# Loading queries and storing outputs of two token groups by one transfer each, in a fused attention and SoLU feed-forward kernel

## The chip, the cores and the metric

The kernel runs on one core of a Trainium2 chip. The metric is the device time of one execution in microseconds (us). TensorE is called PE here, VectorE DVE, ScalarE ACT, GpSimd POOL, and SyncE SP; SP computes nothing and issues nearly all of the DMAs, in the order of the program.

## The reference

Four batches of 12288 queries attend to 768 pooled keys, and each result row goes through a feed-forward layer with a SoLU activation and a layer norm.

```python
kv_pool = kv.reshape(B, H//4, 4, W//4, 4, C).mean(axis=(2, 4))     # B=4, 768 keys of C=128
k = v = kv_pool.reshape(B, -1, C) @ w_sr
s = (q @ k.transpose(0, 2, 1)) / sqrt(C)                           # q: (4, 12288, 128)
a = softmax(s);  x = (a @ v).reshape(B * 12288, C)
h = x @ w_in                                                       # d_ff = 1024
solu = h * softmax(h)
ln = (solu - mean) / sqrt(var + 1e-6) * g_ln
out = ln @ w_out                                                   # (49152, 128), float32
```

## The kernel before

The 49152 query rows are 384 tiles of 128 rows. Four tiles make a group (GT = 4), so there are 96 groups (NG), 24 to a batch. One long loop has 384 slots, and every slot issues one step of each stage of a software pipeline, for tiles that lie further back the later the stage is. In slot t the scores of tile t+1 are computed (`scores_pe`, L386: six matmuls of 384 columns, with the queries split into a high and a low part), the row maximum, exponential and the split of the probabilities of tile t (L402, L403, L407, L415), the product with the values for a whole group in four quarters (`values`, L453), the first feed-forward matmul of tile t-9 (`hidden_pe`, L505), its activation (L513, L529, L543), and the second feed-forward matmul of tile t-13 (`final_pe`, L631: 24 matmuls of 128 columns).

Two operands are turned by DMA transposes that SP issues: the probabilities, 384 KB a tile, from `phl` into `pT` (L422), and the activations, 512 KB a tile, from `uhl` into `uT` (`hidden_turn`, L580). `uhl` is written by two POOL instructions (L560, L566) on `u` of DVE. `final_pe` of a tile stands two slots behind its `hidden_turn`, and `uT` has four buffers. So every slot asks for one transpose of each kind, and over four slots SP also issues one load of queries (`q_load`, L345, 256 KB, at the end of each slot with slot % 4 == 3) and one store of outputs (`final_store`, L685, 256 KB, in each slot with slot % 4 == 1). While batches 1 to 3 are prepared, which is during the three batches before the last, SP also loads raw keys and values, 384 KB at a time (`kv_load`, L216, 64 in all), POOL adds them up (`kv_add`, L227), and some matmuls and transposes of keys are set between the others. In the last batch, from about 1295 us on, none of that is left.

The queries of group g are loaded five slots or more ahead of `q_split` (L354, ACT) and `q_low` (L362, POOL), which split them into `qh` and `ql`; `scores_pe` also reads `qf` itself as bfloat16. `qf` has three buffers of 512 columns, so a load waits until the scores of the group three before have been read. `final_half` (L674, DVE) scales half a group of outputs out of PSUM into `ob`, which has two buffers; the second half is computed in the slot of the store, just ahead of it.

The order of the work on every engine is written out by hand; semaphores are put in by the framework, which gives the DMAs eight completion semaphores in turn. At the start SP's queue holds the two weight matrices, sixteen chunks of the first batch's keys and values (`kv_first_load`, 384 KB each) with the first queries after the sixth chunk, then the queries of groups 1 and 2, and six chunks of batch 1. The last four groups are stored by another function (`final_mul`, `TAIL`), which the change leaves alone.

Of the kernel before, what the change touches and what calls it, by code (L numbers as in the profile page):

```python
# [11 lines left out]
F32 = mybir.dt.float32  # L12
F32R = mybir.dt.float32r
F16 = mybir.dt.float16
BF16 = mybir.dt.bfloat16
# [6 lines left out]
P = 128  # L22
# [10 lines left out]
GT = 4  # L33
GPB = TPB // GT
NG = NT // GT
# [42 lines left out]
def kernel(  # L78
# [15 lines left out]
    nc = tc.nc  # L94

    dmt = ctx.enter_context(tc.tile_pool(name="dmt", bufs=2))
# [45 lines left out]
    state = {}  # L142
# [20 lines left out]
    def kv_first_load(half, c):  # L163

        n = half * 8 + c
        tag, bufs = ("kvc", 9) if n < 9 else ("uT", 4) if n < 13 else ("uhl", 3)
        t = dmt.tile([P, 2, 384], F32, tag=tag, name=f"kv_{half}_{c}", bufs=bufs)
        nc.sync.dma_start(t, kv0[:, 2 * c : 2 * c + 2, half * 384 : half * 384 + 384])
        state["kv0", half, c] = t
# [165 lines left out]
            yield slot, [partial(f, b, half) for f in fs]  # L335


    QL = 1

    def q_load(g):  # L340
        if g >= NG or g % QL:
            return
        b, gb = divmod(g, GPB)
        t = dmt.tile([P, QL * 512], F32, tag="qf", name=f"qf_{g}", bufs=3)
        nc.sync.dma_start(t, qT[b, :, gb * 512 : (gb + QL) * 512])  # L345
        state["qf", g // QL] = t

    def q_split(g):
        if g >= NG:
            return  # L350
        qf = state["qf", g // QL][:, (g % QL) * 512 : (g % QL + 1) * 512]
        qh = grp.tile([P, 512], F32R, tag="qh", name=f"qh_{g}")
        ql = grp.tile([P, 512], BF16, tag="ql", name=f"ql_{g}")
        nc.scalar.copy(qh, qf)  # L354
        state["q", g] = (qh, ql)

    def q_low(g):
        if g >= NG:
            return
        qf = state["qf", g // QL][:, (g % QL) * 512 : (g % QL + 1) * 512]  # L360
        qh, ql = state["q", g]
        nc.gpsimd.tensor_tensor(ql, qf, qh.bitcast(F32), op=ALU.subtract)  # L362

# [3 lines left out]
    def scores_pe(t):  # L367
        g, j = divmod(t, GT)
        b = t // TPB
        qh, ql = state["q", g]  # L370
        qt = state["qf", g // QL].bitcast(BF16).rearrange("p (n two) -> p n two", two=2)[:, :, 1]
        kh, kl, kc = (state[n, b] for n in ("kh", "kl", "kc"))
        ts = slice(j * P, (j + 1) * P)
        s = ps_r.tile([P, 2, 512], F32, tag="r", name=f"s_{t}")
        if t in PY:
            py = s[:, 0, 384:385]
            for half in range(2):
                nc.tensor.matmul(
                    py, onesm, state["kss", PY[t]][:, half : half + 1], start=half == 0, stop=half == 1
                )  # L380
            state["py", PY[t]] = py
        row = [(n, half, *x) for n, x in enumerate(((ql, kc), (qh, kh), (qt, kl))) for half in range(2)]
        if t == 0:
            row = sorted(row[2:4] + row[:2] + row[4:], key=lambda x: x[1])
        for n, half, lh, rh in row:
            nc.tensor.matmul(  # L386
                s[:, half, :384],
                lh[:, ts],
                rh[:, half * 384 : (half + 1) * 384],
                start=n == (t == 0),  # L390
                stop=n == 2,
            )
        state["s", t] = s[:, :, :384]
# [274 lines left out]

    def final_half(g, half):
        _, f = state["f", g]  # L670
        if half == 0:
            state["ob", g, 0] = dmt.tile([P, GT, P], F32, tag="ob", name=f"ob_{g}_0")
        js = slice(half * 2, half * 2 + 2)
        nc.vector.scalar_tensor_tensor(  # L674
            state["ob", g, 0][:, js],
            state["po", g][:, half * 256 : half * 256 + 256].rearrange("p (j c) -> p j c", j=2),
            swi,
            f[:, js].unsqueeze(2).to_broadcast([P, 2, P]),
            op0=ALU.mult,
            op1=ALU.mult,  # L680
        )

    def final_store(g, j0=0, j1=GT):
        t0, n = g * GT + j0, j1 - j0
        nc.sync.dma_start(  # L685
            out[t0 * P : (t0 + n) * P, :].rearrange("(j p) c -> p j c", p=P),
            state.pop(("ob", g, j0)),
        )

    def final_out(g):  # L690
        final_half(g, 1)
        final_store(g)


    ident = const.tile([P, P], F32, name="ident")
# [32 lines left out]
    for n in range(16):  # L728
        if n == OUT_AT:
            nc.sync.dma_start(raw_out, w_out.bitcast(I32))  # L730
        if n == Q_AT:
            q_load(0)
        kv_first_load(*divmod(n, 8))
    q_load(1)
    q_load(2)
    for pos in SOON:
        kv_load(1, pos)
# [36 lines left out]
    nc.vector.tensor_scalar(wsc, wsc, 2.0**14, None, op0=ALU.mult)  # L774
    nc.scalar.activation(w_in_h, wf, AF.Copy, scale=wsc)
    q_split(0)
    q_low(0)
    for f in out_steps[4:]:
        f()
# [63 lines left out]
    def w_low():  # L843
        nc.gpsimd.tensor_tensor(wcl, gw, wch, op=ALU.subtract)

    fill = {
        0: [partial(q_split, 1), partial(q_low, 1), w_mean, w_center],
        1: [busy],
        2: [partial(kv_bound, 0, 1), partial(kv_bound, 0, 2), busy],
# [38 lines left out]
    for b in range(1, B):  # L888
        for k, fs in kv_plan(b):
            plan.setdefault((b - 1) * TPB + k, []).append(fs)  # L890
    scores_pe(0)
    for slot in range(NT):
        i = slot - LH
# [17 lines left out]
        if 0 <= av < NG:  # L911
            values(av, qtr, 0)
        at(slot + 1, scores_pe)
        at_soon(slot - NORM, values_norm)
        at_last(slot - FSC, final_scale)
# [3 lines left out]
        if slot < NT and 0 < qs < slot and (slot - 1 - qs) % GT == 0:  # L919
            q_low(slot // GT + 1)  # L920
# [26 lines left out]
        at_soon(slot - NORM, values_recip_u)  # L947
        at(i + 1, hidden_pe)
        at_last(slot - LO, final_half, 0)
        if slot < NT - 1:  # L950
            at(slot - LO, final_pe)
        if late:
            values(av, qtr, 1)
        at(i - 1, hidden_turn)
        at_last(slot - LO - 1, final_out)
        at_last(slot - XSP, values_out)
        for st in todo:
# [10 lines left out]
        if slot < NT and 0 < qs <= slot and (slot - qs) % GT == 0:  # L968
            q_split(slot // GT + 1)
# [61 lines left out]
```

## Time and profile before

| | |
|---|---|
| three runs, median (lowest to highest) | 1851.75 us (1847.76 to 1853.61) |
| profiled execution, first to last instruction | 1847.1 us; 4.65 us less than the median |
| busy: PE, DVE, ACT, POOL | 1821.1, 1784.9, 1752.8, 1613.8 us |
| DMA | 431.80 MB, mean 234 GB/s |
| DMA issues of SP | 384 `pT`, 378 `uT`, 64 `kv`, 96 `qf`, 97 `out` (two of them smaller) |
| granted TensorE clock | 1.00 in all slices |

The profile is of one execution and has a span alone; its own time with what lies around the span is not listed apart, so the span stands beside the median of the runs. A busy share is the time in which an engine had an instruction in work; ends of matmuls are modelled. For a DMA, the time to landing runs from its issue on SP until its last completion.

### The profile page before, as it was taken

The page shows a single profiled execution, that of the slowest core. Times are in us where ns is not written, and L with a number is a line of the kernel's source. Part 1 is how long each engine was busy: PE and PEld are TensorE (multiplying, and loading weights), DVE is VectorE, ACT ScalarE, POOL GpSimd, SP SyncE. Part 2 cuts the span into 40 slices and gives each one's busy share as a digit, 9 for nine tenths or more (in the row PEclk, how much of TensorE's full clock was granted, in tenths as well). Part 3 has the DMA queues.
Part 4 walks back from the last instruction along what each step waited for, and adds up shares of the span by engine and source line. Part 5 has one row for each costly group of instructions (what it writes and reads, how often), then busy time and mean ns, then how long its engine had stood idle before and what let it go on. Part 6 is the DMA issues. An engine that isn't in the chain of part 4 may idle for free.

```text
span 1847.1 us, 43152 instructions
## 1 busy us (share of the span) xinstructions
PE 1821.1 (99%) x15717; PEld 1179.2 (64%) x15718; DVE 1784.9 (97%) x2729; ACT 1752.8 (95%) x3148; POOL 1613.8 (87%) x1392
## 2 busy tenths in 40 slices
PE   8999999999999999999999999999999999999999
PEld 4566666666666666666666666666666666666666
DVE  7999999999999999999999999999999999999998
ACT  6999999999999999999999999999999999999998
POOL 3899889899998999989988899989888888888887
PEclk9999999999999999999999999999999999999999
DMA  8999999999999999999999999999999999999998
GB/s 300 208 238 233 229 245 234 236 240 245 232 234 240 244 238 241 235 233 238 235 233 234 247 241 241 238 236 231 227 217 230 233 228 223 230 227 231 224 223 179
DMA packets 1473253, 431.80 MB, mean 234 GB/s; under 512 B 1400977, under 2 KB 1454353, under 8 KB 1472785
## 3 DMA queue, kind: packets, MB, share of 16 engines
q1 hardware_dynamic: 1472752, 428.98, 114.1%
q8 instruction: 124, 2.03, 0.5%
q14 instruction: 89, 0.72, 0.1%
q10 hardware_dynamic: 288, 0.07, 0.0%
HBM read 52.50 MB, written 25.17 MB: 42 GB/s over the span
## 4 chain that ended last, share of the span: by engine, by line
PE 63%; DVE 13%; ACT 7%; POOL 7%; issue 7%; DMA 3%; DVEq 0%; POOLq 0%; ACTq 0%
PE o L631 19%; PE h L505 18%; PE xa L453 13%; PE s L386 13%; DVE junkd L513 3%; DVE nm L402 3%; POOL uhl L566 3%; DVE phl L415 2%; ACT e L529 2%; DMA pT<-phl 2%; ACT junk L603 2%; POOL uhl L560 2%; ACT phl L407 2%; DVE u L543 1%; DVE ob L674 1%
## 5 line engine op out<-in xcount | busy, mean ns | idle before, releaser
L566 POOL TENSOR_TENSOR uhl<-u,uhl 128x1024 f16<-128x1024 f32 x382 | 815.1, 2134 | 31.7 <-ACT uhl L558 0.2
L631 PEld LDWEIGHTS <-uT 128*128 128x128 f16 x9072 | 537.1, 98 | 91.9 <-DMA uT<-uhl 7.0
L631 PE MATMUL o<-wch,uT 128*128 128x128 f16 x6048 | 568.0, 219 | 1.3 <-DMA uT<-uhl 1.3
L631 PE MATMUL o<-wcl,uT 128*128 128x128 f16 x3024 | 525.9, 219 | 0.0
L560 POOL TENSOR_SCALAR uhl<-u 128x1024 f16<-128x1024 f32 x377 | 393.5, 1044 | 136.2 <-DVE u L543 131.1
L543 DVE SCALAR_TENSOR_TENSOR u<-h,rz,e 128x1024 f32<-128x1024 f32 x384 | 491.2, 1279 | 16.0 <-ACT e L529 3.6
L513 DVE TENSOR_SCALAR_CACHE_REDUCE junkd<-h,rz 128x1024 bf16<-128x1024 f32 x384 | 491.5, 1280 | 1.4 <-PE h L505 1.0
L529 ACT ACTIVATE e<-h,nm,rz 128x1024 f32<-128x1024 f32 x384 | 459.0, 1195 | 1.0 <-DVE junkd L513 1.0
L603 ACT ACTIVATE junk<-u,su 128x1024 bf16<-128x1024 f32 x384 | 437.8, 1140 | 0.2 <-DVE u L543 0.2
L402 DVE TENSOR_REDUCE nm<-s 128x1 f32<-128x768 f32 x384 | 365.7, 952 | 23.3 <-PE s L386 20.8
L453 PE MATMUL xa<-pT,vh 128*128 128x512 f16 x1152 | 373.5, 379 | 6.6 <-DMA pT<-phl 4.0
L403 ACT ACTIVATE s<-s,nm 128x768 f32<-128x768 f32 x384 | 335.9, 875 | 41.9 <-DVE nm L402 37.1
L415 DVE SCALAR_TENSOR_TENSOR phl<-s,phl 128x768 f16<-128x768 f32 x384 | 366.3, 954 | 4.5 <-ACT phl L407 4.3
L407 ACT ACTIVATE phl<-s 128x768 f16<-128x768 f32 x384 | 311.0, 810 | 11.7
L505 PEld LDWEIGHTS <-xh 128*128 128x128 f16 x1536 | 144.8, 97 | 191.7 <-issue 26.7
L386 PE MATMUL s<-kh,qh 128*128 128x384 f32 x768 | 248.0, 404 | 0.1
L505 PE MATMUL h<-w_in_h,xh 128*128 128x512 f16 x768 | 228.2, 379 | 3.5 <-DVE rz L487 2.4
L505 PE MATMUL h<-w_in_h,xl 128*128 128x512 f16 x768 | 228.4, 379 | 0.0
L505 PE MATMUL h<-w_in_l,xh 128*128 128x512 f16 x768 | 228.3, 379 | 0.0
L453 PE MATMUL xa<-pT,vl 128*128 128x512 f16 x576 | 218.3, 379 | 0.0
L386 PE MATMUL s<-kc,ql 128*128 128x384 bf16 x768 | 187.8, 326 | 7.4 <-DVE phl L415 4.4
L386 PE MATMUL s<-kl,qf 128*128 128x384 bf16 x768 | 192.2, 332 | 0.1
(127 smaller groups left out, 1707.2 us busy)
## 6 DMA issues: line engine op xcount, KB each, us to landing
kv<-in_kv_dram SPq DMA_DIRECT2D x64, 384.0 KB, 4.3
qf<-in_q_dram SPq DMA_DIRECT2D x96, 256.0 KB, 3.3
out_dram<-ob SPq DMA_DIRECT2D x95, 256.0 KB, 2.8
pT<-phl SPq DMA_TRANSPOSE x384, 3.8
uT<-uhl SPq DMA_TRANSPOSE x378, 4.4
raw_in<-in_moe_w_in_dram SPq DMA_DIRECT2D x1, 1024.0 KB, 5.4
raw_out<-in_moe_w_out_dram SPq DMA_DIRECT2D x1, 1024.0 KB, 8.6
out_dram<-ob SPq DMA_DIRECT2D x1, 192.0 KB, 2.0
```

The source lines that it names most:

```text
L386: nc.tensor.matmul(s[:, half, :384], lh[:, ts], rh[:, half * 384 : (half + 1) * 384], start=n == (t == 0), stop=n == 2,)
L402: nc.vector.tensor_reduce(nm, s, axis=AX.XY, op=ALU.max, negate=True)
L415: nc.vector.scalar_tensor_tensor(phl[:, 1], state.pop(("s", t)), SC, phl[:, 0], op0=ALU.mult, op1=ALU.subtract)
L453: nc.tensor.matmul(xa, v[:, c, :], pT[:, :, a * NKC + c, :], start=n == 0, stop=n == len(seq) - 1)
L505: nc.tensor.matmul(h[:, hs], lh[:, ts], rh[:, hs], start=n == 0, stop=n == 2)
L513: nc.vector.tensor_scalar(junk, state["h", t], state["rz", g][1][:, j : j + 1], None, op0=ALU.mult, op1=ALU.min, accum_out=nm,)
L529: nc.scalar.activation(e, state["h", t], AF.Exp, bias=nm, scale=state["rz", g][0][:, js], accum_out=state["z2", g][:, js],)
L543: nc.vector.scalar_tensor_tensor(u, state.pop(("h", t)), state["rz", g][2][:, j : j + 1], state.pop(("e", t)), op0=ALU.mult, op1=ALU.mult, ...
L560: nc.gpsimd.tensor_scalar(uhl[:, 0, :], u, 1.0, 1.0, op0=ALU.mult, op1=ALU.mult)
L566: nc.gpsimd.tensor_tensor(uhl[:, 1, :], u, uhl[:, 0, :], op=ALU.subtract)
L603: nc.scalar.activation(junk, u, AF.Square, scale=-float(DFF), bias=su, accum_out=state["v3", g][:, j : j + 1],)
L631: nc.tensor.matmul(po[:, ts], uT[:, a * NFC + c, :], w[:, c, :], start=start, stop=stop)
```

## The change

`q_load` loads the queries of two groups at once, 512 KB, into a tile of 1024 columns with two buffers (before: 512 columns and three). It is called in the same places and does nothing for an odd g. Only groups 0 and 1 are still loaded apart, into the two halves of one tile. The outputs of two groups are gathered in a tile `ob2` of 512 KB with one buffer (before: 256 KB and two), and one DMA stores them behind the second half of the odd group. Thus the loads of the loop stand in the slots with slot % 8 == 7, and the stores in those with slot % 8 == 5. `qf` takes 2048 bytes more of each partition, `ob2` 4096 more beside `ob`, which the tail still uses.

```diff
-    def q_load(g):
-        if g >= NG or g % QL:
+    def q_load(g, n=2):
+        if g >= NG or n == 2 and g % 2:
             return
         b, gb = divmod(g, GPB)
-        t = dmt.tile([P, QL * 512], F32, tag="qf", name=f"qf_{g}", bufs=3)
-        nc.sync.dma_start(t, qT[b, :, gb * 512 : (gb + QL) * 512])
-        state["qf", g // QL] = t
+        if g % 2 == 0:
+            state["qf", g // 2] = dmt.tile([P, 1024], F32, tag="qf", name=f"qf_{g}", bufs=2)
+        nc.sync.dma_start(
+            state["qf", g // 2][:, g % 2 * 512 : (g % 2 + n) * 512], qT[b, :, gb * 512 : (gb + n) * 512]
+        )
...
     def final_half(g, half):
         _, f = state["f", g]
-        if half == 0:
-            state["ob", g, 0] = dmt.tile([P, GT, P], F32, tag="ob", name=f"ob_{g}_0")
+        if half == 0 and g % 2 == 0:
+            state["ob2", g // 2] = dmt.tile([P, 2 * GT, P], F32, tag="ob2", name=f"ob2_{g}", bufs=1)
         js = slice(half * 2, half * 2 + 2)
+        j0 = g % 2 * GT + half * 2
         nc.vector.scalar_tensor_tensor(
-            state["ob", g, 0][:, js],
+            state["ob2", g // 2][:, j0 : j0 + 2],
...
     def final_out(g):
         final_half(g, 1)
-        final_store(g)
+        if g % 2:
+            t0 = (g - 1) * GT
+            nc.sync.dma_start(
+                out[t0 * P : (t0 + 2 * GT) * P, :].rearrange("(j p) c -> p j c", p=P),
+                state.pop(("ob2", g // 2)),
+            )
...
         if n == Q_AT:
-            q_load(0)
+            q_load(0, 1)
         kv_first_load(*divmod(n, 8))
-    q_load(1)
+    q_load(1, 1)
     q_load(2)
```

## Rows read from the trace of the kernel before

**Rows 1.** Busy by stretch: us, engine's busy us (instructions), granted clock, DMA share, GB/s.
```profile
185.00:1295.00 1110.00, 1100.09 (x9577) 713.90 (x9575) 1081.20 (x1655) 1062.34 (x1913) 1006.51 (x870) 1.00 1.19 238
1295.00:1800.00 505.00, 504.41 (x4416) 328.74 (x4415) 497.69 (x763) 488.17 (x872) 426.94 (x360) 1.00 1.13 226
```

**Rows 2.** Row maximum (L402, one a slot) by stretch: DVE's busy us and count.
```profile
185.00:1295.00 1110.00, 223.96 (x235) 1.00 1.19 238
1295.00:1800.00 505.00, 103.75 (x109) 1.00 1.13 226
```

**Rows 3.** Waits of the whole span: who, for whom, us in total, times, longest us.
```profile
PEld L631 <- DMA uT<-uhl: 7.0, 14, 1.0
...
PEld L453 <- DMA pT<-phl: 4.2, 8, 1.4
PE xa L453 <- DMA pT<-phl: 4.0, 8, 1.0
...
PE xa L453 <- DVE ob L674: 2.2, 2, 1.1
...
PE o L631 <- DMA uT<-uhl: 1.3, 4, 0.5
```

**Rows 4.** Instructions on tile uT, 185 to 1295 us alone: idle before them.
```profile
  DMA uT<-uhl: 8.3, 18
```

**Rows 5.** Timeline in the stretch with key loads: start us, us, engine, line.
```profile
926.21 0.53 SPq L685 DMA_DIRECT2D out_dram<-ob  x1
...
927.20 2.13 POOL L566 TENSOR_TENSOR uhl<-u,uhl 128x1024 f16<-128x1024 f32 x1
...
932.31 0.47 DVE L674 SCALAR_TENSOR_TENSOR ob<-o,swi,f 128x256 f32<-128x256 f32 x1
...
934.96 2.27 SPq L580 DMA_TRANSPOSE uT<-uhl  x1
...
937.32 0.53 SPq L345 DMA_DIRECT2D qf<-in_q_dram  x1
...
937.96 2.48 SPq L580 DMA_TRANSPOSE uT<-uhl  x1
```

**Rows 6.** Timeline in the last batch.
```profile
1522.86 2.13 POOL L566 TENSOR_TENSOR uhl<-u,uhl 128x1024 f16<-128x1024 f32 x1
...
1525.02 1.61 SPq L580 DMA_TRANSPOSE uT<-uhl  x1
```

**Rows 7.** Half microseconds around one load of queries (last column GB/s).
```profile
956.80:957.30 0.50, 0.50 (x4) 0.10 (x1) 0.50 (x3) 0.50 (x1) 0.50 (x1) 1.00 1.28 290
957.30:957.80 0.50, 0.50 (x4) 0.24 (x4) 0.50 (x3) 0.50 (x4) 0.50 (x1) 1.00 0.87 190
957.80:958.30 0.50, 0.50 (x4) 0.26 (x3) 0.50 (x1) 0.50 (x2) 0.50 (x2) 1.00 0.56 62
958.30:958.80 0.50, 0.50 (x6) 0.26 (x5) 0.50 (x2) 0.30 (x2) 0.50 (x1) 1.00 0.50 123
```

**Rows 8.** Half a microsecond inside a store.
```profile
908.00:908.50 0.50, 0.50 (x8) 0.32 (x5) 0.50 (x3) 0.50 (x1) 0.50 (x1) 1.00 1.12 335
```

**Rows 9.** Four microseconds of loads back to back, at the start.
```profile
8.00:12.00 4.00, 3.88 (x13) 1.90 (x11) 3.86 (x5) 1.42 (x2) 0.00 (x0) 1.00 1.03 417
```

**Rows 10.** DMA issues: count, KB each, median us to landing.
```profile
kv<-in_kv_dram SPq DMA_DIRECT2D x64, 384.0 KB, 4.3
qf<-in_q_dram SPq DMA_DIRECT2D x96, 256.0 KB, 3.3
out_dram<-ob SPq DMA_DIRECT2D x95, 256.0 KB, 2.8
```

**Rows 11.** Timeline of ACT at the start, idle time and its releaser in brackets.
```profile
17.67 0.60 ACT L354 CAST qh<-qf 128x512 fp32r<-128x512 f32 x1
...
27.99 0.48 ACT L196 CAST kh<-pk 128x384 fp32r<-128x384 f32 x1 [3.46 <-PE pk L185]
```

**Rows 12.** Timeline of PE at the start.
```profile
27.50 0.63 PE L386 MATMUL s<-kh,qh 128*128 128x384 f32 x1
```

More of the change, by code (lines that the diff above doesn't have):

```diff
@@ L335, in kv_plan @@
             yield slot, [partial(f, b, half) for f in fs]
-    QL = 1
-    def q_load(g):
-        if g >= NG or g % QL:
+    def q_load(g, n=2):
+        if g >= NG or n == 2 and g % 2:
             return
         b, gb = divmod(g, GPB)
-        t = dmt.tile([P, QL * 512], F32, tag="qf", name=f"qf_{g}", bufs=3)
-        nc.sync.dma_start(t, qT[b, :, gb * 512 : (gb + QL) * 512])
-        state["qf", g // QL] = t
+        if g % 2 == 0:
[3 more added lines that the diff above has]
+        )
     def q_split(g):
@@ L350, in q_split @@
             return
-        qf = state["qf", g // QL][:, (g % QL) * 512 : (g % QL + 1) * 512]
+        qf = state["qf", g // 2][:, g % 2 * 512 : g % 2 * 512 + 512]
         qh = grp.tile([P, 512], F32R, tag="qh", name=f"qh_{g}")
@@ L359, in q_low @@
             return
-        qf = state["qf", g // QL][:, (g % QL) * 512 : (g % QL + 1) * 512]
+        qf = state["qf", g // 2][:, g % 2 * 512 : g % 2 * 512 + 512]
         qh, ql = state["q", g]
@@ L370, in scores_pe @@
         qh, ql = state["q", g]
-        qt = state["qf", g // QL].bitcast(BF16).rearrange("p (n two) -> p n two", two=2)[:, :, 1]
+        qf = state["qf", g // 2][:, g % 2 * 512 : g % 2 * 512 + 512]
+        qt = qf.bitcast(BF16).rearrange("p (n two) -> p n two", two=2)[:, :, 1]
         kh, kl, kc = (state[n, b] for n in ("kh", "kl", "kc"))
```

## The prediction

> **What bounds the kernel now.** I read the busy time by stretch first. From 1295 us on PE stands still for 0.59 of 505 us; between 185 and 1295 us, where keys of the next batches are loaded and prepared, for 9.91 of 1110 us [rows 1]. The granted clock is 1.00 in both. So PE sets the pace, and in the last batch it loses nothing that a change of DMAs could give back. Then I counted slots by the row maximum, which runs once in each: 1110 / 235 = 4.723 us a slot against 505 / 109 = 4.633 us [rows 2]. The difference, 0.09 us x 235 = 21 us, is partly the keys' own matmuls and partly waiting.
>
> The list of waits says for what. PE waits for transposes that have not landed: `xa` for `pT` 4.0 us, `o` for `uT` 1.3 us, and weight loads, which overlap matmuls, 7.0 and 4.2 us for the same two [rows 3]. The view of `uT` between 185 and 1295 us alone has all 18 of its waits, 8.3 us [rows 4]; in the last batch there is none. Of the 9.91 us, 2.2 us are a wait for DVE [rows 3], and some 1.7 us I put to smaller ones; that leaves about 6.0 us for transposes.
>
> Why they are late is seen in the timeline. In the last batch POOL ends its half of a tile at 1522.86 + 2.13 = 1524.99 us and SP takes up the transpose at 1525.02 us, at once [rows 6]. With key loads, POOL ends at 927.20 + 2.13 = 929.33 us and that tile's transpose (POOL's instructions and the transposes are matched by their order in the run) starts at 934.96 us, 5.6 us late [rows 5]. SP's queue is behind there, though an ordinary DMA holds SP for only 0.53 us, 0.64 us until the next instruction (937.32 to 937.96 us) [rows 5]. The queue is behind because the DMA engines are full: transposes run at 290 GB/s, which is what a stretch of them shows, and the mean is 238 GB/s with a share of 1.19 [rows 1, 7]. In the last batch the share is 1.13, and there the backlog is gone.
>
> **The change, part by part.** 47 of 96 loads and 46 of 97 stores go away as instructions, no bytes do. Between 185 and 1295 us it is 235 / 8 = 29 of each.
>
> *SP's time.* 93 x 0.64 us = 60 us of SP [rows 5]. I cost it at nothing: SP stands behind full DMA engines, and what it saves it waits at the next transpose, whose 2.27 and 2.48 us in these rows are mostly such waiting. If the DMA engines ran dry while SP issues, it would be worth up to 0.64 us a transfer; the rate of 290 GB/s just ahead of a load, and 335 GB/s inside a store, speak against that [rows 7, 8].
>
> *The loads.* When the DMA engines turn from transposes to a load, the rate falls: 190, 62 and 123 GB/s in three half microseconds, against 290 [rows 7]. The missing bytes are (100 + 228 + 167) x 0.5 = 248 KB, or 248 / 290 = 0.85 us of DMA time. One of two such holes goes away with a pair, if the hole does not grow with the size. That it does grow, I can't exclude: 128 KB more make a key load land 1.0 us later than a query load (4.3 against 3.3) [rows 10], as much as two loads would cost. So a pair saves between 0 and 0.85 us; I take 0.4 us, in the middle, since rows 7 and rows 10 point opposite ways. 29 x 0.4 = 12 us of DMA time. PE gets of this only what it now waits, 6.0 us at most, and only at tiles where the backlog was the cause; I take half, -3 us. Outside the stretch it is worth nothing, as PE does not wait there.
>
> *The stores.* A store runs at 335 GB/s and has no hole [rows 8], so merging saves no DMA time: 0.
>
> *Longer transfers.* Against that, the transposes behind a merged transfer find 262 KB more ahead of them, 262 / 290 = 0.90 us, once in eight slots for loads and once for stores; in the other four slots they find 0.90 us less. A transpose with spare time pays nothing for it. 18 of some 235 tiles and 8 of 59 groups have none [rows 3, 4]; that is 26 of 470 transposes, 5.5%. With three transposes behind each of 58 merged transfers, 58 x 3 x 5.5% = 10 are hit, at half of 0.90 us: +4.5 us; the relief in the other half of the groups can give back half of that. I take +2 us. The bounds are 0 (the relief is as large as the loss) and 58 x 0.90 / 3 = 17 us (a third of all merged transfers find a transpose without spare time).
>
> The Trainium skill has a rule that speaks against this part: DMA: Bandwidth & Descriptors, section Queues, rings and completion order, has descriptors of one queue consumed in ring order on each DMA engine. Rows 5 agree, since the transpose at 937.96 us stands behind a load on the same queue and still follows it; by the rule alone, without any spare time in the tiles, the cost would be 58 x 0.90 = 52 us.
>
> *Buffers.* `ob2` has one buffer, so DVE's first half of an even group waits until the store of the pair before has landed. That store is issued in the fifth slot of eight, and the next write is three slots later, as now between neighbouring groups: SP issues at 926.21 us, it lands some 2.8 us later [rows 10], at 929.0 us, and DVE writes next at 932.31 us [rows 5]. 0.90 us more leave 2.4 us: nothing. `qf` holds two pairs; the load of a pair waits for the scores of the second group of the pair that it replaces, which are read one slot ahead, as now. The first load of a pair is needed as early as before and the second one four slots later: nothing. POOL, DVE and ACT do the same instructions.
>
> *The start.* Groups 0 and 1 share a tile, filled by two loads. `q_split(0)` at 17.67 us [rows 11] reads only the first half. PE's first score starts at 27.50 us while ACT writes the second half of the same `kh` tile at 27.99 us [rows 11, 12], so waits are set by the part of a tile that is touched: 0. The load of groups 2 and 3 puts 256 KB ahead of keys that are needed much later: 0.
>
> **The sum.** Profiled span 1847.1 us, and 4.65 us to the median of 1851.75 us; - 3 (holes) + 2 (longer transfers) + 0 for the rest = 1850.75 us. I say 1850.5 us: no change that can be measured. A measurement of this kernel tells about 0.3%, 5.6 us, from no change (the three runs alone lie 5.85 us apart).
>
> **The rivals.**
>
> *Faster, the DMA engines were the bound.* For it: where SP is behind, each slot costs 0.09 us more, and the holes' full price is 29 x 0.85 = 25 us of DMA time, more than PE loses. Then the 6.0 us go, and up to some 4 us of the 21 us that are neither idle time nor the keys' work: 1841.8 to 1846 us. Against it: PE waits for transposes at 26 of 470 places, so most of the backlog is in spare time already; the last batch, with a share of 1.13, can gain nothing. The Trainium skill, page SBUF — State Buffer, section The DMA setup-cost knee, counts a fixed cost of some 2 us for every transfer, which would be an estimate of 93 x 2 = 186 us here if all of it stood in the path. The 3.3 us in which 262 KB land [rows 10] do have such a part, but the next transpose is issued 0.64 us after the load [rows 5], so it overlaps; by the trace it is not in the path. Chance 24%.
>
> *Slower, a burst in front of tight transposes.* After the 512 KB load of every eighth slot a key load of 384 KB often follows in the next slot, with a single transpose between, and the store of 512 KB comes in one piece before the pair of `pT` transposes. It decides when spare time of the transposes behind is under 0.90 us at more than 12 of the 58 bursts: 13 x 0.90 / 2 - 2 = 4 us is about the noise; at a third of them with the full 0.90 us it is +17 us, 1869 us, and at a sixth some +9 us, 1860 us. For it: the backlog of 5.6 us. Against it: the amount of DMA work between two `pT` pairs falls in one half of the eight slots by as much as it rises in the other. Chance 15%.
>
> *Slower, a new wait.* If waits went by whole tiles, `q_split(0)` would wait for a load that stands behind ten more chunks: 11 transfers, 4.2 MB, at 417 GB/s [rows 9], 10 us, less the 3.46 us that ACT is idle later [rows 11]: +6.6 us, 1858 us. Or `ob2` holds up DVE: it decides when SP is more than 2.4 us later than in rows 5, and 10 such of 1 us cost 10 us. Chance 5% for both.
>
> **How the numbers follow.** No measurable change has 56%, faster 24%, slower 15 + 5 = 20%. The likeliest case alone reaches from 1846.2 to 1857.3 us. For 8 in 10 I go down to the end of the faster case, 1842 us, and up to a sixth of the bursts, 1860 us.
>
> **What would show it.** In the profile after: 49 loads and 51 stores; `qf` to landing between 4 and 5.5 us; one hole of about 0.85 us per load if holes do not grow, twice as long if they do. Waits of PE for `uT` and `pT` stay at about 26, moved to the slots behind loads and stores of pairs. PE idle between 185 and 1295 us stays within 10 +- 4 us. No wait of DVE L674 for a store, and ACT L354 starts at 17.7 us. I am wrong if a slot of the last batch changes from 4.633 us, or if PE's idle time between 185 and 1295 us falls under 5 us or rises over 15 us.

## The result and the profile after

The changed kernel takes 1869.12 us (median of 4 runs, 1865.48 to 1870.29) against 1850.53 us of the kernel before beside it: ratio 1.0104, 95% interval 1.0088 to 1.0119, 19 us slower. I had said 1850.5 us and no measurable change. The profiled execution spans 1868.5 us.

First the busy time by stretch, as in [rows 1].

```profile
185.00:1295.00 1110.00, 1082.98 (x9390) 698.50 (x9388) 1063.14 (x1620) 1042.93 (x1874) 988.69 (x851) 1.00 1.19 233
1295.00:1800.00 505.00, 504.42 (x4419) 329.09 (x4417) 497.26 (x766) 488.74 (x874) 430.80 (x364) 1.00 1.14 228
```

PE stands still for 27.0 us of the first stretch and 0.58 us of the second; before it was 9.9 and 0.59 us. The last batch has not changed. The DMA engines are as busy as before in the first stretch (1.19) and move less, 233 and not 238 GB/s. The row maximum, which runs once a slot, says how much work got done there: 231 slots, where [rows 2] have 235. Four slots at 4.72 us are 19 us, as much as the whole loss.

```profile
185.00:1295.00 1110.00, 220.02 (x231) 1.00 1.19 233
```

The list of waits of the whole span, to be held against [rows 3]:

```profile
PEld L632 <- DMA uT<-uhl: 34.8, 42, 2.1
...
PE o L632 <- DMA uT<-uhl: 16.8, 21, 1.6
POOL uhl L561 <- DMA uT<-uhl: 14.0, 16, 1.8
...
PE xa L454 <- DMA pT<-phl: 3.4, 8, 0.9
DVE ob L676 <- PE o L632: 3.3, 5, 1.1
PEld L454 <- DMA pT<-phl: 3.3, 5, 1.1
```

The waits for `pT` are as they were. Those for `uT` have grown from 7.0 and 1.3 us to 34.8 and 16.8 us. POOL has a wait that was not there: it can't write `uhl` until the transpose three tiles back has read it. DVE does not wait for a store anywhere, so the single buffer of `ob2` costs nothing, as predicted. The view of `uT` between 185 and 1295 us, as in [rows 4], has 61 waits where there were 18. Its second part tells who waited:

```profile
  DMA uT<-uhl: 49.6, 61
...
  PEld L632: 33.5, 41
  PE o L632: 16.1, 20
```

Weight loads (PEld) run beside matmuls, so only the last line is idle time of PE: 16.1 us, against 1.3 us before [rows 3]. A weight load and a matmul that wait for the same transpose are counted apart. Counted by transpose, the 61 waits are for 41, and the 18 of before for 14. Of the 41, 23 are the first or second `uT` transpose behind a merged load; they hold 14.2 of PE's 16.1 us.

SP's timeline around one of the merged loads (start us, us):

```profile
275.98 1.72 SPq L581 DMA_TRANSPOSE uT<-uhl  x1
277.79 0.53 SPq L344 DMA_DIRECT2D qf<-in_q_dram  x1
278.42 3.60 SPq L581 DMA_TRANSPOSE uT<-uhl  x1
282.07 0.57 SPq L216 DMA_DIRECT2D kv<-in_kv_dram  x1
282.75 1.39 SPq L423 DMA_TRANSPOSE pT<-phl  x1
284.23 3.11 SPq L581 DMA_TRANSPOSE uT<-uhl  x1
```

The transpose right behind the load holds SP for 3.60 us; in [rows 5] it was 2.48 us. The next one, behind a key load, takes 3.11 us. The issues have the sizes that the diff asks for; a merged load lands after 4.9 us where a single one took 3.3 us [rows 10]:

```profile
kv<-in_kv_dram SPq DMA_DIRECT2D x64, 384.0 KB, 4.4
qf<-in_q_dram SPq DMA_DIRECT2D x47, 512.0 KB, 4.9
out_dram<-ob SPq DMA_DIRECT2D x46, 512.0 KB, 3.4
```

Half microseconds from the first packet of that load on, as in [rows 7] (last column GB/s; transposes alone run at 290):

```profile
279.14:279.64 0.50, 0.50 (x4) 0.22 (x3) 0.50 (x3) 0.50 (x3) 0.50 (x1) 1.00 1.31 206
279.64:280.14 0.50, 0.50 (x5) 0.20 (x3) 0.50 (x1) 0.50 (x2) 0.50 (x2) 1.00 0.87 156
280.14:280.64 0.50, 0.50 (x5) 0.26 (x4) 0.50 (x2) 0.30 (x2) 0.50 (x1) 1.00 0.71 188
280.64:281.14 0.50, 0.50 (x12) 0.50 (x11) 0.50 (x1) 0.50 (x1) 0.41 (x1) 1.00 0.89 328
```

### The profile page after: what moved, and what is told of

The parts are those of the page before. It is cut to its first block, busy times and chain, and to the rows that moved or that the text cites. A ratio compares the mean times of both kernels' runs of the same rounds, so it can differ in the third digit from the quotient of the medians.

```text
span 1868.5 us, 42925 instructions
## 1 busy us (share of the span) xinstructions
PE 1826.0 (98%) x15718; PEld 1177.9 (63%) x15718; DVE 1787.1 (96%) x2729; ACT 1753.5 (94%) x3148; POOL 1616.1 (86%) x1392
## 4 chain that ended last, share of the span: by engine, by line
PE 53%; DVE 15%; DMA 8%; POOL 8%; issue 8%; ACT 7%; DVEq 0%; POOLq 0%; ACTq 0%
PE o L632 16%; PE h L506 14%; PE s L387 11%; PE xa L454 11%; DMA uT<-uhl 7%; DVE junkd L514 4%; DVE nm L403 3%; DVE phl L416 3%; POOL uhl L567 3%; ACT e L530 2%; POOL uhl L561 2%; ACT junk L604 2%; DVE u L544 2%; ACT phl L408 2%; DVE ob L676 1%
## 5 line engine op out<-in xcount | busy, mean ns | idle before, releaser
L632 PEld LDWEIGHTS <-uT 128*128 128x128 f16 x9072 | 535.5, 98 | 113.4 <-DMA uT<-uhl 34.8
L632 PE MATMUL o<-wch,uT 128*128 128x128 f16 x6048 | 568.2, 219 | 17.6 <-DMA uT<-uhl 16.8
```

What stands on the lines that cost most here:

```text
L632: nc.tensor.matmul(po[:, ts], uT[:, a * NFC + c, :], w[:, c, :], start=start, stop=stop)
```

## The experiments

A ratio is that of a run to the kernel before on the same chip; its 95% interval stands in brackets.

**Which part.** First the two halves of the change one by one, the loads cut in two, and the tiles alone.

*Paired loads, stores as before:* `final_half` and `final_out` as in the kernel before.

> Queries in pairs as in the change, outputs stored one group at a time as before. Theory 1 (the paired load is the burst that makes the next two activation transposes late): nearly the whole loss stays, 1864 to 1870 us, and TensorE waits for uT in the same two slots of eight as after the change. Theory 2 (the paired store, or its single buffer, is to blame): 1848 to 1853 us, as before. Theory 3 (both together only, or the new places of the tiles in memory): between the two, 1854 to 1862 us.

1870.29 us, 1.0115 [1.0098, 1.0132]. The loads alone make the whole loss.

*Paired stores, loads as before.*

> Outputs of two groups stored by one transfer, queries loaded one group at a time as before. Theory 1 (paired loads are to blame): no loss, 1847 to 1854 us. Theory 2 (paired stores): 1864 to 1870 us. Theory 3 (both together): 1852 to 1858 us.

1851.76 us, 1.0014 [1.0003, 1.0025]. The stores cost 0.6 to 4.6 us by the interval.

*Paired loads by two DMAs in the same place of the queue:*

```diff
-        nc.sync.dma_start(
-            state["qf", g // 2][:, g % 2 * 512 : (g % 2 + n) * 512], qT[b, :, gb * 512 : (gb + n) * 512]
-        )
+        for k in range(n):
+            nc.sync.dma_start(
+                state["qf", g // 2][:, (g % 2 + k) * 512 : (g % 2 + k + 1) * 512],
+                qT[b, :, (gb + k) * 512 : (gb + k + 1) * 512],
+            )
```

> The queries of two groups are loaded in the same place of the queue as in the change, but by two DMAs of 256 KB right behind each other; stores as before. If the amount of data in one place of the queue does the harm, and not the size of one transfer or its longer rows, the time is that of the run with paired loads only, within 4 us. If the single large transfer does it (4096-byte rows, one long hole at its start), the loss shrinks by half or more, to under 1859 us.

1851.01 us, 1.0010 [0.9998, 1.0023]: -0.4 to +4.3 us, against some 20. The same bytes in the same slot lose little or nothing as long as two DMAs carry them. My first theory, a burst of bytes, falls with this run.

*The pair's tile, each half loaded in its old slot.*

> The tile of two groups and its two buffers as in the change, with each half loaded by its own DMA in the slot where it was loaded before; stores as before. Only the tile's shape, its place in memory and the waits that hang on it differ from the kernel before. Theories 1 and 2: the time of before, 1847 to 1854 us. Theory 3 (layout or buffers): part of the loss is there, over 1857 us.

1850.56 us, 1.0007 [0.9997, 1.0018]. Neither the tile nor its buffers nor its place cost anything that can be measured.

*The change with both pairs, the load by two DMAs.*

> The change as it is, with paired stores, but each pair of queries by two DMAs of 256 KB behind each other. If the paired load in one DMA is the whole cause and the paired stores cost nothing: 1848 to 1856 us. If pairing the stores adds to a burst of loads: 1857 to 1866 us.

1852.74 us, 1.0016 [1.0005, 1.0027]: the change without its one large load is the paired stores' run.

**Long rows or one large DMA.** A DMA of 512 KB has rows of 4096 bytes, two of 256 KB have 2048. Space between the halves of the tile, which are then addressed as `[:, g % 2, :512]`, keeps the rows short in one DMA:

```diff
-            state["qf", g // 2] = dmt.tile([P, 1024], F32, tag="qf", name=f"qf_{g}", bufs=2)
+            state["qf", g // 2] = dmt.tile([P, 2, 520], F32, tag="qf", name=f"qf_{g}", bufs=2)
```

> Queries of two groups by one DMA of 512 KB as in the run with paired loads only (1870 us), but into a tile with 32 bytes of space between the two halves, so that the rows of the transfer are 2048 bytes and not 4096. Stores as before. Theory rows (long rows make the DMA engines slow to come back from the load): the loss is gone, 1847 to 1855 us, and the next transpose lands some 6 us after the issue of the load. Theory transfer (one completion of 512 KB, whatever its rows): 1864 to 1872 us and 7.7 us.

2060.18 us, 1.1143 [1.1114, 1.1171]: neither theory. Three more runs make the key rows and the query rows of the kernel before short in the same way, with 32 bytes behind each half:

> The kernel before, with the key loads of 384 KB into tiles with space between their halves, so that their rows are 1536 bytes and not 3072. Theory rows: the hole that a key load makes gets smaller, PE waits less between 185 and 1295 us, 1838 to 1846 us. Theory transfer: 1847 to 1854 us, no change.

2076.05 us, 1.1235 [1.1218, 1.1253].

> The kernel before, with each query load of 256 KB in rows of 1024 bytes and not 2048, by the same means; ScalarE and GpSimd read the same numbers in two pieces of a row. Theory rows: a little faster if shorter rows go on helping below 2048 bytes, 1842 to 1848 us. Theory transfer, or a threshold above 2048 bytes: 1847 to 1854 us.

2077.92 us, 1.1244 [1.1221, 1.1267].

> The kernel before with both key rows of 1536 and query rows of 1024 bytes. Theory rows: the two gains add up, 1834 to 1844 us, bounded below by the 4.633 us a slot of the last batch, some 1830 us. Theory transfer: 1847 to 1854 us.

1852.55 us, 1.0020 [1.0008, 1.0032], with both edits at once. What sets these four apart is how far the space shifts the tiles that lie behind it: 128, 576, 192 and 768 bytes. Only the last is a multiple of 256. So the next run shifts everything by 128 bytes and does nothing else:

```diff
-    dmt.tile([P, 96], F32, tag="pad", name="pad", bufs=1)
+    dmt.tile([P, 128], F32, tag="pad", name="pad", bufs=1)
```

> The kernel before with a first pad of 512 bytes a partition and not 384: every tile shifts by 128 bytes, nothing else changes. Theory shift (the transposes run at some 210 and not 290 GB/s when their tiles leave their places within 256 bytes): 2040 to 2090 us. If the earlier runs were slow by their rows or the split tiles: 1847 to 1854 us.

2072.47 us, 1.1197 [1.1178, 1.1216]. The slow runs above were slow by the shift, and say nothing of rows. The busy view of this run between 185 and 1295 us:

```profile
185.00:1295.00 1110.00, 999.23 (x8447) 626.49 (x8445) 964.49 (x1460) 941.47 (x1683) 892.26 (x767) 0.99 1.12 210
```

210 GB/s on average and not 238 [rows 1], and PE idle for 111 us. Then the row question again, with 256 bytes of space:

> As the run with paired loads in rows of 2048 bytes, with 256 bytes of space after each half and not 32, so that every tile stands at the same place within 256 bytes as before. Theory rows: 1847 to 1855 us, as with two DMAs in the same place. Theory transfer (a single DMA of 512 KB does it, whatever its rows): 1864 to 1872 us. Over 2000 us if the space itself, and not the shift of the tiles, made the earlier run slow.

1869.45 us, 1.0100 [1.0080, 1.0120]. With rows of 2048 bytes one DMA of 512 KB loses as much. Half microseconds from its first packet on, and below them those of the run with two DMAs:

```profile
316.60:317.10 0.50, 0.50 (x4) 0.27 (x3) 0.50 (x1) 0.50 (x1) 0.50 (x1) 1.00 1.67 134
317.10:317.60 0.50, 0.50 (x4) 0.13 (x2) 0.50 (x3) 0.50 (x2) 0.50 (x1) 1.00 0.32 106
317.60:318.10 0.50, 0.50 (x4) 0.20 (x3) 0.50 (x2) 0.50 (x4) 0.50 (x1) 1.00 0.90 111
318.10:318.60 0.50, 0.50 (x4) 0.27 (x3) 0.50 (x2) 0.35 (x1) 0.50 (x2) 1.00 0.58 221
```

```profile
316.33:316.83 0.50, 0.50 (x4) 0.17 (x3) 0.50 (x3) 0.50 (x1) 0.50 (x1) 1.00 0.96 197
316.83:317.33 0.50, 0.50 (x4) 0.24 (x4) 0.50 (x2) 0.50 (x4) 0.50 (x1) 1.00 0.79 233
317.33:317.83 0.50, 0.50 (x4) 0.20 (x2) 0.50 (x1) 0.46 (x1) 0.50 (x2) 1.00 0.92 340
317.83:318.33 0.50, 0.50 (x7) 0.35 (x6) 0.50 (x2) 0.34 (x1) 0.50 (x1) 1.00 0.83 298
```

The hole is more than 1.5 us long with one DMA, and with two the rate is back over 290 GB/s after the first microsecond. The same, averaged over all loads between 185 and 1290 us (packets of the trace summed by their start, in half microseconds from the load's first packet), and the median time from the load's issue to the landing of the transpose right behind it:

```
                                    GB/s in the first four half us   transpose behind lands after
before, one group (58; 59 landings)     185  248  286  218             5.9 us
two DMAs of 256 KB (29 pairs)           224  285  289  313             6.7 us
one DMA of 512 KB, the change (29)      194  149  191  248             7.2 us
one DMA of 512 KB, loads only (29)      194  155  183  202             7.7 us
one DMA, rows of 2048 bytes (29)        138  136  187  229             7.1 us
```

The first 2 us are not the whole of it. With two DMAs the rate falls later, to 208 and 168 GB/s in the next two half microseconds. Over 4 us the mean is 214 GB/s for the change and 242 GB/s for two DMAs; over the whole stretch before it was 238 [rows 1]. So behind the load of one group the rate is about that mean (234 in the first 2 us), behind two DMAs it is no lower, and behind the single large one it is.

The packets of a load tell more. From the start of its first to the start of its last they take 1.5 us for one DMA of 256 KB, 2.2 us for a key load of 384 KB and 2.9 to 3.1 us for one DMA of 512 KB, with rows of 2048 bytes as of 4096 (medians of the traces). That is 171 to 182 GB/s at every size. Two DMAs of 256 KB behind each other take 2.4 us together, 220 GB/s.

*Short key rows with 256 bytes of space*, the same question for a DMA of 384 KB:

> The kernel before with key loads in rows of 1536 bytes and not 3072, with space of 256 bytes that shifts no tile within 256 bytes. Theory rows, if the hole grows with the row at every length: the hole of a key load shrinks, 1838 to 1846 us. If only rows above 3072 bytes are slow, or the transfer's size counts: 1847 to 1854 us.

1851.02 us, 0.9999 [0.9989, 1.0010]. Rows do not matter here either.

**Smaller DMAs.** If the hole grows with the bytes of one DMA, key loads in two pieces must gain.

```diff
-        nc.sync.dma_start(
-            t, kv[b - 1, r, :, two * NK : (two + 1) * NK].rearrange("p (h k) -> p h k", h=2)
-        )
+        for h in range(2):
+            k = two * NK + h * 384
+            nc.sync.dma_start(t[:, h, :], kv[b - 1, r, :, k : k + 384])
```

> The kernel before, each key load of 384 KB issued as two DMAs of 192 KB behind each other, into the same tile. Theory hole (one DMA's hole grows with its bytes: 0.75 us until the full rate for 256 KB, 1.25 us for 384 KB, some 2 us for 512 KB): the hole shrinks to some 0.6 us, PE waits less for transposes, 1840 to 1847 us. Theory threshold (only transfers above 384 KB do harm): 1847 to 1854 us. Theory issue time (SP has no time to spare): slower by 64 x 0.64 us at most, up to 1890 us.

1846.21 us, 0.9985 [0.9976, 0.9994]: 2.8 us faster, 1.1 to 4.4 by the interval. The packets of a key load take 1.9 us and not 2.2. The waits on `uT` between 185 and 1295 us fall from 8.3 us [rows 4] to

```profile
  DMA uT<-uhl: 3.5, 9
```

This is what the theory asks for, but one profile does not prove it: PE's idle time in the stretch is 9.2 us against 9.9, and the run with the tile alone has 21 such waits, 13.1 us, at the time of before.

*The query loads of 256 KB in two pieces as well:*

> As the run with key loads in two DMAs, and each query load of 256 KB as two of 128 KB too. Theory hole: faster still by a little, 1836 to 1846 us. Theory threshold: 1847 to 1854 us. Theory issue time: up to 1950 us.

1854.87 us, 1.0030 [1.0019, 1.0041]: 8.7 us slower than with the key loads alone. There was little to win, as two DMAs of 128 KB take 1.4 us and one of 256 KB 1.5 us. What the 96 further DMAs cost, SP's time or something else, no run separates.

**Is the key load behind it needed?** `slot = max(ADDS[pos] - 8, ...) + 2` moves every key load by two slots, so none follows a merged load directly.

> Queries in pairs by one DMA of 512 KB, stores as before (1870 us without more), and every key load moved by two slots, so that it no longer follows a paired load with one transpose between. Theory hole: about half of the loss or more goes, by the run with the same move of the key loads in the kernel before, since the paired load meets transposes with more time to spare. Theory transfer alone (the paired load makes the next two transposes late whatever comes behind): the difference to that run stays 17 to 22 us.

1877.85 us, 1.0157 [1.0142, 1.0173].

> The kernel before with every key load two slots later, ahead of the pair of pT transposes: the run that the one with paired loads and moved keys is set against. Either theory: 1845 to 1860 us, since the key load now stands before the transposes with the least time to spare.

1858.38 us, 1.0048 [1.0031, 1.0065]. Between the two lie 19.5 us; with the key loads in their old places the paired loads cost 21.6 us. The key load behind is not needed for the loss. The waits are others here: PE stands still for 34.0 and 18.2 us between 185 and 1295 us, but `uT` has only 27 and 7 waits. How the delay reaches PE in this order I did not follow.

**Order in the queue, or the DMA engines' rate.** The loads of the loop go out by ScalarE, `(nc.sync if g < 3 else nc.scalar).dma_start(...)`, into another queue, so that no transpose stands behind them.

> Paired loads in one DMA of 512 KB as in the run with paired loads only (1870 us), but issued by ScalarE into its own DMA queue, in the same place of the program; stores as before. Theory order (the transposes are late since they stand behind the load in one queue): most of the loss goes, 1848 to 1858 us. Theory rate (the DMA engines themselves are slow while the large load is under way, whoever issued it): 1862 to 1875 us.

1890.30 us, 1.0218 [1.0197, 1.0239]: slower than either theory, and now in the last batch too, where PE is idle for 12.5 us, 10.2 of them in five waits for `pT`:

```profile
185.00:1295.00 1110.00, 1078.00 (x9324) 696.97 (x9322) 1057.03 (x1611) 1035.59 (x1861) 980.29 (x845) 1.00 1.19 232
1295.00:1800.00 505.00, 492.50 (x4289) 320.04 (x4288) 484.71 (x742) 475.70 (x852) 418.89 (x357) 1.00 1.16 220
```

> The version that could beat both kernels: key loads in two DMAs of 192 KB (1846 us) and the queries one group at a time as before, issued by ScalarE into its own queue. Theory order: 1838 to 1845 us, as no transpose stands behind a query load. Theory rate: 1844 to 1850 us; slower than that if ScalarE pays for the 94 issues.

1853.13 us, 1.0026 [1.0015, 1.0037]. Taking the loads out of the transposes' queue makes it worse, for small loads and for large ones. ScalarE does not pay for the issues: each takes 0.33 us, and all 46 of the run with pairs, and 92 of 93 here, lie under an instruction that it was running anyway. So the order in one queue does not explain the loss by itself; whether it has a share, these runs do not tell, as the second queue has a price of its own.

## Why the prediction was wrong

**What bounds the kernel** held. The loss lies where keys are loaded and SP's queue is behind: four slots fewer between 185 and 1295 us. In the last batch PE's idle time went from 0.59 to 0.58 us.

**Longer transfers: the step that failed.** I let the transposes behind a merged load come 0.90 us later, its further 262 KB at the transposes' own 290 GB/s, and gave +2 us for it. The trace shows them 1.3 to 1.8 us later (7.2 and 7.7 against 5.9 us). A load by one DMA goes at some 175 GB/s, so its packets take 1.4 to 1.6 us more. With two DMAs it is 0.8 us, as I had said for the bytes alone, and the time changes by -0.4 to +4.3 us. So spare time covers most of a delay of 0.8 us, and not one of 1.3. Instead of 10 transposes that cost 0.45 us each, 41 - 14 = 27 more were waited for, and PE's idle time rose by 27.0 - 9.9 = 17.1 us, 0.63 us for each: 2.7 times as many, and each 1.4 times as dear. The count took a transpose behind a load to be as likely without spare time as any other, and it read the 18 waits of [rows 4] as 18 tiles, where they are for 14 transposes.

**The loads: the saving is not there.** I took -3 us because one of two holes goes away. In the table above, the bytes missing from 290 GB/s in the first 2 us are (96 + 141 + 99 + 42) x 0.5 = 189 KB for one DMA of 512 KB, against (105 + 42 + 4 + 72) x 0.5 = 112 KB for one of 256 KB, of which a pair of groups had two. So the hole grows almost with the bytes, and comes in one place. The hole in [rows 7], 248 KB, was that of one load, and twice the mean. The row that told of the growth was mine too, 1.0 us more to landing for 128 KB more [rows 10]; I used it to bound the saving, and did not add the larger hole to the delay of the transposes behind. Two DMAs in one place have the smallest hole in the first 2 us, (66 + 5 + 1 - 23) x 0.5 = 25 KB.

**The rival that came nearest** was the burst in front of tight transposes: a third of the bursts, +17 us, against 18.6 us measured. It named the place, but its causes, the bytes and the key load behind, are not what the runs show, and its 58 bursts count the stores, which cost almost nothing. That its number fits is luck.

That transposes stand behind the load in one queue, which I had cited from the Trainium skill (DMA: Bandwidth & Descriptors, section Queues, rings and completion order), agrees with the timeline. It is not enough to explain the loss: taken out of the queue, the loads cost 20 us more. The other page of the Trainium skill that I had cited, SBUF — State Buffer, section The DMA setup-cost knee, advises the largest single transfer where DMA is the bound; here the measurement speaks against it, at 512 KB by 1.0% and at 384 KB by 0.15%.

**The rest.** SP's time at nothing held: the run with paired stores has 46 issues fewer and is no faster. Stores at nothing was nearly right, +0.14% (0.03 to 0.25). `ob2`, `qf` and the start at nothing held: DVE waits for no store, the tile alone is at 1.0007, and `q_split(0)` starts at 17.73 us (17.67 us before). 49 loads, 51 stores and 4.9 us to landing came as said. PE's idle time of 27.0 us is far over the 15 us at which I had called myself wrong.

**What stays open:** why one DMA goes at some 175 GB/s between transposes, whatever its size, where two behind each other reach 220. Rows, tile, place and the key load behind are out, and another queue did not cure it. What differs is that the reads of two DMAs are asked for 0.58 us apart (median of the run with two DMAs); that is argued, not shown.

## What to carry to other kernels

Where the DMA engines are nearly full and others wait on short transfers, merging loads removes instructions that were not on the path, and can make one delay that is longer than the spare time behind it. Before counting saved issues, look at the rate of the DMA engines in the half microseconds behind a load, at how long the load's own packets take, and at the spare time of what follows. Price a load by its own rate in that place, not by that of the transfers around it. Bytes in one place of the queue are not the same as bytes in one DMA: here 512 KB and 384 KB were better cut in two, 256 KB was not. When an edit changes the size of a buffer, keep the shift of the tiles behind it a multiple of 256 bytes, as far as this kernel shows, or a comparison measures the shift.

## What the hardware showed unexpectedly

- A shift of all tiles by 128 bytes a partition costs 12.0%; shifts of 128, 192 and 576 bytes through other edits cost 11.4 to 12.4%, one of 768 bytes 0.2%. The stretch with key loads then runs at 210 and not 238 GB/s. The Trainium skill, DMA: Bandwidth & Descriptors, section DMA Transpose (X-bar), asks a transpose for 32-byte alignment; 128 bytes keep that, and the time is lost all the same. Which of the tiles has to stand at a multiple of 256 bytes no run tells apart.
- One DMA from HBM in the midst of transposes lowers the DMA engines' rate for a time that grows with its bytes, at 2048-byte rows as at 4096: its packets go at 171 to 182 GB/s at 256, 384 and 512 KB. Loads back to back at the start, of 256 KB to 1 MB and with no transposes between, run at 417 GB/s [rows 9].
- Packets of 8 or 16 KB on the instruction queues are followed by a deeper hole than the loads are on average: over 92 places between 185 and 1295 us of the kernel before, the mean of all other packets is 193, 79, 122 and 154 GB/s in the four half microseconds from such a packet on. The change has as many of these packets (127, before 128), so they do not make its loss. That they cause the hole is not tested.
- Loads of 512 KB in ScalarE's queue beside transposes in SP's cost some 20 us more than in SP's own queue (1890.30 against 1870.29 us), and loads of 256 KB some 7 us (1853.13 against 1846.21 us, or 1.0026 against 0.9985, both with the key loads cut). Why is not shown.
